# Attention features and a gated network on one core: the matrix S loaded as 16 columns and spread on the chip, values with 33 columns a head, a new order

## The chip, the cores and the metric

The kernel runs on one core of one Trainium2 chip. The metric is the device time in microseconds (us) of one execution, the median of three runs. Engines are PE (TensorE, matmuls), DVE (VectorE), ACT (ScalarE), POOL (GpSimd) and SP (SyncE, which issues most transfers).

## The reference, cut to what matters

```python
B, H, S, D = 4, 4, 1088, 32          # q, k, v: (B, H, S, D); S1, S2: (8, 32)
def phi(x):                          # 64 features of a row of 32
    a = np.einsum('rd,bhsd->bhsr', S1, x)
    b = np.einsum('rd,bhsd->bhsr', S2, x)
    return np.einsum('bhsi,bhsj->bhsij', a, b).reshape(*x.shape[:-1], 64)
q_p, k_p = phi(q), phi(k)
kv = np.einsum('bhsf,bhsd->bhfd', k_p, v)
z = np.sum(k_p, axis=2)
attn = np.einsum('bhsf,bhfd->bhsd', q_p, kv) / (np.einsum('bhsf,bhf->bhs', q_p, z)[..., None] + 1e-06)
x = attn.transpose(0, 2, 1, 3).reshape(4352, 128)
xn = x / np.sqrt(np.mean(x * x, axis=-1, keepdims=True) + 1e-06) * rms_g
g = xn @ w_gate                      # w_gate, w_val: (128, 1536); w_out: (1536, 128)
out = (g / (1 + np.exp(-g)) * (xn @ w_val)) @ w_out
```

S1, S2 and the weights come as 64-bit floats and are made into 32-bit ones on the chip.

## The kernel before, in words

The 4352 tokens are nine chunks (eight of 512, one of 256). For each of the four batches `kside(b)` projects the keys with S, takes the outer products of the two projections (`phi`, 64 features a head), and sums features times values into `kv` (line 531, the key-value products). The values `vt` have VA = 34 columns a head: 32 values, a one (its sum is z), and a zero. Batch 0 does this in groups of 1, 3, 3 and 2 key tiles of 128 rows: key products on PE (L519), a copy by ACT (`both`, L344), the outer product by POOL or DVE (L452), then L531. Batches 1 to 3 project turned (L497, four strips of 32 columns side by side on PE).

For each chunk `qside(c)` does the same with queries: chunks 0 and 1 with L594, the outer product into `at` (L452), transposes on PE (L602) and a copy into `phiq`; later chunks with L622 and a way through DRAM (`far`). Then come the numerator and denominator (L678), the division and the mean of squares on DVE, a power on POOL (`rstd`), the scaling of x on ACT or DVE, transposes on PE (L758), and the split of x into x_hi and x_lo.

A slot (c, j) is 128 of the 1536 hidden columns for one chunk: three matmuls each for the gate `g_ps` and the value `v_ps` (L802: x_hi with w_hi and w_lo, x_lo with w_hi), a silu on ACT into `s`, h = v*s on DVE, h split into h_hi and h_lo, and three matmuls into `o_ps` (L840). `weights(j)` loads 384 KB of 64-bit weights, casts the upper parts (`w_top`, L401), joins them (`w_full`, L396) and splits them (`w_hi`, `w_lo`). Gate and value have two banks each; `att` has three and `o_ps` one.

S as the kernel needs it, `sblk`, is block-diagonal: 128 rows (head and d), 64 columns (head, S1 or S2, r), zeros outside a head's own block. The host writes all of it, as 64-bit words; `to_f32` casts the upper halves (`s_top`) and joins them with the rest (`s_raw`) into `sblk`.

Nothing decides at run time. Every operation is a numbered task with one engine, or a choice of engines that the string `ON` makes; the list `ORDER` says in which sequence tasks are put down, and the numbers behind it (as LAGS, ASK, FETCH, FETCH_AT) are a model's from which slots of buffers and filler matmuls follow. Each engine runs its own instructions in that sequence. Fillers (L382) are products with zeros: eight at the start, and one wherever the model sees PE idle.

```python
load(P * NB * 16, lambda: nc.sync.dma_start(out=s_raw.bitcast(U16)[:, 1:4 * NB + 1], in_=sw.bitcast(U16)), ["s_raw"])
to_f32(NB, lambda: sblk, lambda: s_raw, lambda: s_top, ["s_raw", "table"], ["s_top"], ["sblk"])
```

Of the kernel before, what the change touches and what calls it, by code (L numbers as in the profile page):

```python
# [22 lines left out]
R = 8  # L23
F = R * R
NT = B * S
P = 128
# [9 lines left out]
VA = D + 2  # L36
# [3 lines left out]
LAGS = (210, 240, 740)  # L40
# [48 lines left out]
"""  # L89
ON = (  # L90
    "dapapadaddaadaadddaaaaapapdapapaadaadaadaapaadaadaadaadaddaadppddaapaadaaddadadadadadadadpdddaadddaaapapadadapapaadapapd"
    "dapapadapadapdpddddpadaaddadaapadaddpddadddadapadapddddadpadaadapaddpadapadddapapddadaaadpdaadpadadapddadddddapdpddddddd"
    "ddaaaapapapddapapdpdpddadaddpadadddaaaddddpapddadaddpadddapaddaddddaaddddpddapadadapadaddddpadpadddadadadadddapdda"
)
ATT = 3
# [856 lines left out]
```

## Time and profile before

| | |
|---|---|
| median of 3 runs | 252.21 us (252.2 to 252.3) |
| the profiled execution | 252.34 us, its span 250.4 us |
| busy in the span | PE 246.5, DVE 180.6, ACT 132.8, POOL 81.9 us |
| instructions | 5878 |
| moved by DMA | 25.55 MB, 20.40 MB read from HBM |
| first product with S, first up product, last product | starts at 4.21, 16.58 and 246.39 us (a group of eight, 1.05 us) |
| single durations on ACT | kv copy 0.21, copy of 512 columns 0.59, x_hi of 256 columns 0.46 us |
| single durations on DVE | join of 384 columns 0.55, kv copy 0.22, copy of 128 columns 0.28, eight columns 0.17 us |

The span runs from the first instruction to the last; the time has some 2 us around it. A timeline row is the start, the duration, the engine, the line, the operation, what it writes and reads, the shape, and how many records it covers; an idle time before it and what ended that stand in brackets. A 32-bit product is two records, and a product with rounded operands (hi or lo) one. A PE record reaches to the modelled end, so records overlap: the pace of PE is the distance from start to start.

### The profile page before, as it was taken

What the parts mean: (1) busy time and instruction counts of PE and PEld (TensorE: products, weight loads), DVE (VectorE), ACT (ScalarE), POOL (GpSimd) and SP (SyncE); (2) the same over time, 40 slices, a digit from 0 to 9 for tenths busy, and PEclk for the clock granted to TensorE, in tenths of its full rate; (3) what the DMA queues carried; (4) which work ended last, traced back from release to release, by engine and by line L of the source; (5) the groups of instructions that cost most, each with busy time, mean ns of one, the idle gap of its engine ahead of it and who ended that gap; (6) DMA issues with size and microseconds to landing.
All of it is one profiled execution on the core that took longest, in us unless ns stands there. A gap on an engine that the chain in (4) does not pass through costs nothing.

```text
span 250.4 us, 5878 instructions
## 1 busy us (share of the span) xinstructions
PE 246.5 (98%) x2244; PEld 198.7 (79%) x2244; DVE 180.6 (72%) x410; ACT 132.8 (53%) x287; POOL 81.9 (33%) x80
## 2 busy tenths in 40 slices
PE   8999999999999999999999999999999999999995
PEld 5977788777888788878888788888888888888894
DVE  1899998789467887575587678855678576765672
ACT  3686988564444747353445643553356464355351
POOL 4447031343664223223550403265332203132201
PEclk9999999999999999999999999999999999999999
DMA  6989892552371332321610254251002102010010
GB/s 238 359 265 343 269 251 91 158 152 45 108 205 41 86 98 77 105 86 34 183 34 1 47 153 112 45 149 61 3 0 46 41 3 43 21 63 3 0 42 21
DMA packets 19691, 25.55 MB, mean 102 GB/s; under 512 B 3152, under 2 KB 11472, under 8 KB 19664
## 3 DMA queue, kind: packets, MB, share of 16 engines
q1 hardware_dynamic: 19232, 24.54, 33.3%
q10 hardware_dynamic: 432, 0.66, 0.7%
q8 instruction: 17, 0.28, 0.4%
q14 instruction: 10, 0.08, 0.1%
HBM read 20.40 MB, written 4.78 MB: 101 GB/s over the span
## 4 chain that ended last, share of the span: by engine, by line
PE 98%; DVE 0%; issue 0%
PE v_ps L802 29%; PE g_ps L802 29%; PE o_ps L840 28%; PE att L678 3%; PE att L531 2%; PE o_ps L382 2%; PE att L622 1%; PE o_ps L531 1%; PE att L594 1%; PE att L758 1%; PE att L497 1%; PE g_ps L678 0%; PE att L602 0%; PE v_ps L678 0%; PE att L821 0%; PE g_ps L519 0%
## 5 line engine op out<-in xcount | busy, mean ns | idle before, releaser
L811 ACT ACTIVATE s<-g_ps 128x512 f32<-128x512 f32 (+1 forms) x108 | 61.0, 574 | 71.4 <-PE g_ps L802 38.1
L814 DVE TENSOR_TENSOR h<-v_ps,s 128x512 f32<-128x512 f32 (+2 forms) x110 | 69.8, 647 | 40.0 <-PE v_ps L802 27.7
L832 POOL TENSOR_TENSOR h_lo<-h,h_hi 128x512 fp32r<-128x512 f32 (+1 forms) x42 | 52.9, 1267 | 104.5 <-DVE h_lo L832 43.9
L350 ACT CAST h_hi<-h 128x512 fp32r<-128x512 f32 (+1 forms) x70 | 41.3, 601 | 19.9 <-DVE h L814 17.4
L832 DVE TENSOR_TENSOR h_lo<-h,h_hi 128x512 fp32r<-128x512 f32 (+1 forms) x64 | 41.4, 652 | 5.5 <-ACT h_hi L350 3.6
L802 PE MATMUL v_ps<-x_hi,w_hi 128*128 128x512 f32 (+1 forms) x110 | 41.9, 381 | 0.0
L802 PE MATMUL g_ps<-x_hi,w_hi 128*128 128x512 f32 (+1 forms) x110 | 41.9, 381 | 0.0
L802 PE MATMUL v_ps<-x_hi,w_lo 128*128 128x512 f32 (+1 forms) x110 | 41.6, 378 | 0.0
L802 PE MATMUL g_ps<-x_hi,w_lo 128*128 128x512 f32 (+1 forms) x110 | 41.5, 378 | 0.0
L802 PE MATMUL g_ps<-x_lo,w_hi 128*128 128x512 f32 (+1 forms) x110 | 41.5, 379 | 0.0
L802 PE MATMUL v_ps<-x_lo,w_hi 128*128 128x512 f32 (+1 forms) x110 | 41.3, 378 | 0.0
L840 PE MATMUL o_ps<-h_hi,w_hi 128*128 128x512 f32 (+1 forms) x106 | 40.9, 386 | 0.0
L840 PE MATMUL o_ps<-h_hi,w_lo 128*128 128x512 f32 (+1 forms) x106 | 40.8, 385 | 0.0
L840 PE MATMUL o_ps<-h_lo,w_hi 128*128 128x512 f32 (+1 forms) x106 | 40.8, 385 | 0.0
L802 PEld LDWEIGHTS v_ps<-x_hi,w_hi 128*128 128x128 f32 x110 | 20.6, 188 | 5.0 <-DVE w_lo L436 0.5
L802 PEld LDWEIGHTS g_ps<-x_hi,w_hi 128*128 128x128 f32 x110 | 20.7, 188 | 4.6
L802 PEld LDWEIGHTS v_ps<-x_hi,w_lo 128*128 128x128 f32 x110 | 20.7, 188 | 4.3
L802 PEld LDWEIGHTS g_ps<-x_hi,w_lo 128*128 128x128 f32 x110 | 20.7, 188 | 4.3
L802 PEld LDWEIGHTS g_ps<-x_lo,w_hi 128*128 128x128 f32 x110 | 20.6, 188 | 4.2
L802 PEld LDWEIGHTS v_ps<-x_lo,w_hi 128*128 128x128 f32 x110 | 20.5, 188 | 4.1
L840 PEld LDWEIGHTS o_ps<-h_lo,w_hi 128*128 128x128 f32 x106 | 19.9, 188 | 4.4
L840 PEld LDWEIGHTS o_ps<-h_hi,w_hi 128*128 128x128 f32 x106 | 19.9, 188 | 4.2
(112 smaller groups left out, 246.9 us busy)
## 6 DMA issues: line engine op xcount, KB each, us to landing
w_raw<-w SPq DMA_DIRECT2D x12, 384.0 KB
bt<-far SPq DMA_DIRECT2D x24, 128.0 KB
at<-far SPq DMA_DIRECT2D x12, 256.0 KB
outT<-o_sb SPq DMA_DIRECT2D x16, 128.0 KB
q<-qT SPq DMA_DIRECT2D x7, 256.0 KB
turned<-xq SPq DMA_DIRECT2D x24, 64.0 KB
xt<-turned SPq DMA_DIRECT2D x6, 256.0 KB
vt<-v SPq DMA_DIRECT2D x4, 272.0 KB
```

Source lines behind the costliest of these rows:

```text
L350: "act": on_act(n, lambda: nc.scalar.copy(out=out(), in_=in_()), True),
L382: nc.tensor.matmul(out=warm[:1, :cols], lhsT=zeros[:, :1], rhs=zeros[:, :cols], start=True, stop=True)
L497: nc.tensor.matmul(out=pair[p]()[a * D:(a + 1) * D, :g], lhsT=sblk[p * HALF:(p + 1) * HALF, p * NB // 2:(p + 1) * NB // 2], rhs=kt()[p * H ...
L531: nc.tensor.matmul(out=kvv[r0:r0 + wide, h // 2, :], lhsT=phi()[:, t, h * F + f:h * F + f + wide], rhs=vt()[:, t, h, :], start=(t == 0 and ...
L594: nc.tensor.matmul(out=ab()[hf * HALF:(hf + 1) * HALF, t * HALF:(t + 1) * HALF], lhsT=q()[:, s1:s1 + HALF], rhs=sblk, start=True, stop=True,)
L622: nc.tensor.matmul(out=accs[p]()[a * D:(a + 1) * D, :m], lhsT=sab[rows, p].rearrange("p c o r -> p (c o r)"), rhs=q()[rows, a * m:(a + 1) ...
L678: nc.tensor.matmul(out=nv[n0:n0 + wide, t, p, :], lhsT=phi()[:, p, l0:l0 + wide], rhs=kvs[(s0 + l0) // S][:, p, :], start=True, stop=True,)
L802: nc.tensor.matmul(out=acc()[:, cs], lhsT=wt[:, j, i3, :], rhs=x()[:, cs], start=(i == 0), stop=(i == 2))
L811: act(n, lambda: nc.scalar.activation(out=s()[:, :n], in_=gps()[:, :n], func=AF.Silu), cols(gps, whole[0]), [s])
L814: cs.stop - cs.start, lambda cs=cs: nc.vector.tensor_tensor(out=h()[:, cs], in0=vps()[:, cs], in1=s()[:, cs], op=ALU.mult),
L832: eng.tensor_tensor(out=h_lo()[:, :n], in0=h()[:, :n], in1=h_hi().bitcast(F32)[:, :n], op=ALU.subtract)
L840: nc.tensor.matmul(out=o_ps()[:, :n], lhsT=wt[:, j, 2, :], rhs=x()[:, :n], start=first and i == 0, stop=last and i == 2,)
```

## The change

The host now sends S1 and S2 side by side, 16 columns for each of the 128 rows (the same 32 rows for each head): 16 KB instead of 64. The chip joins these 16 columns (`s_one`) and multiplies them, repeated for four heads, with `own`, which is one where the row belongs to the column's head and zero elsewhere. `own` is made by five memsets on DVE at the start. Values have 33 columns a head. All tasks behind the join have a number one higher, and the order, the choice of engines and some numbers of the model are new. The lines move by six to ten: L519 is L529, L531 L541, L594 L604, L602 L612, L622 L632, L678 L688, L497 L507, L758 L768, L802 L812.

```diff
-VA = D + 2
+VA = D + 1
-LAGS = (210, 240, 740)
+LAGS = (120, 240, 700)
...
 ORDER = """
-1 0 2 6 9 3 14 10 15 4 32 33 7 37 16 5 64 34 18 38 19 12 26 27 22 20 146 39 28 147 11 23 24 151 35 40 41 65 17 13 148 21 25 36 29 152 153 149 66 72
+1 0 2 3 4 7 15 16 17 11 10 19 8 12 38 33 23 20 21 34 27 24 35 18 25 39 40 6 66 28 5 67 22 36 29 14 68 37 71 13 41 73 69 42 74 26 70 65 30 31 32 80
...
-AHEAD, FETCHED, BLOCK, ASK, FETCH = 62, 210, 128, 2600, 2400
+AHEAD, FETCHED, BLOCK, ASK, FETCH = 62, 210, 128, 3300, 2800
+LATE = 150
...
-    s_raw = const.tile([P, 2 * NB + 2], U32, name="s_raw")
+    s_raw = const.tile([P, 4 * R + 2], U32, name="s_raw")
...
-    s_top = const.tile([P, NB], U32, name="s_top")
+    s_top = const.tile([P, 2 * R], U32, name="s_top")
+    s_one = const.tile([P, 2 * R], F32, name="s_one")
+    own = const.tile([P, H], F32, name="own")
+    nc.vector.memset(own, 0.0)
+    for h in range(H):
+        nc.vector.memset(own[h * D:(h + 1) * D, h:h + 1], 1.0)
...
-    load(P * NB * 16, lambda: nc.sync.dma_start(out=s_raw.bitcast(U16)[:, 1:4 * NB + 1], in_=sw.bitcast(U16)), ["s_raw"])
+    load(P * 2 * R * 16, lambda: nc.sync.dma_start(out=s_raw.bitcast(U16)[:, 1:8 * R + 1], in_=sw.bitcast(U16)), ["s_raw"])
...
-    to_f32(NB, lambda: sblk, lambda: s_raw, lambda: s_top, ["s_raw", "table"], ["s_top"], ["sblk"])
+    to_f32(2 * R, lambda: s_one, lambda: s_raw, lambda: s_top, ["s_raw", "table"], ["s_top"], ["s_one"])
+    dve(NB, lambda: nc.vector.tensor_tensor(
+        out=sblk.rearrange("p (h x) -> p h x", h=H), in0=s_one.unsqueeze(1).to_broadcast([P, H, 2 * R]),
+        in1=own.unsqueeze(2).to_broadcast([P, H, 2 * R]), op=ALU.mult,
+    ), ["s_one"], ["sblk"], True)
```

The order below is that of each engine's own instructions: line, operation, what it writes and reads, the shape, and how often. First the start of PE, before: after the fillers a key tile (`kt`), query blocks (`q_109` is chunk 0, `q_113` chunk 1) with fillers between them, and the other key tiles.

```order
L382 MATMUL o_ps_97<-const-float32-0.0 1x96
L519 MATMUL g_ps_124<-sblk,kt_106 64x64 x2
L382 MATMUL o_ps_97<-const-float32-0.0 1x32
L594 MATMUL att_130<-sblk,q_109 64x64 x4
L382 MATMUL o_ps_97<-const-float32-0.0 1x128
L594 MATMUL att_144<-sblk,q_109 64x64 x4
L519 MATMUL v_ps_151<-sblk,kt_106 64x64 x6
L519 MATMUL v_ps_162<-sblk,kt_106 64x64 x4
L519 MATMUL g_ps_170<-sblk,kt_106 64x64 x6
L594 MATMUL att_179<-sblk,q_113 64x64 x4
L594 MATMUL att_186<-sblk,q_113 64x64 x4
L602 MATMUL g_ps_193<-ident,at_149 128x128 x4
```

The same place now. Behind the last of these rows stand 15 more key-value products, the transposes of chunk 0, twenty key-value products, and only then the two query blocks of chunk 1.

```order
L388 MATMUL o_ps_104<-const-float32-0.0 1x128 x8
L529 MATMUL g_ps_132<-sblk,kt_113 64x64 x2
L529 MATMUL v_ps_137<-sblk,kt_113 64x64 x6
L604 MATMUL att_150<-sblk,q_116 64x64 x4
L604 MATMUL att_159<-sblk,q_116 64x64 x4
L529 MATMUL g_ps_165<-sblk,kt_113 64x64 x6
L529 MATMUL v_ps_174<-sblk,kt_113 64x64 x4
L541 MATMUL o_ps_183<-vt_120,phi_148 64x33
```

So the key tiles moved ahead of the queries, the fillers between them are gone, and the first sixteen key-value products stand ahead of the transposes; before, all 36 stood behind them. DVE's first instructions show the new step and who makes the first large product; before:

```order
L357 MEMSET mhalf 128x4
L404 CAST s_top<-s_raw 128x64
L396 SCALAR_TENSOR_TENSOR sblk<-s_raw,s_top 128x64
L452 TENSOR_TENSOR at_149<-att_130,both_141 128x512
L452 TENSOR_TENSOR at_149<-att_144,both_158 128x512
L452 TENSOR_TENSOR phi_138<-v_ps_162,both_177 128x512
```

DVE now (the cast of `s_top` stands on ACT, behind its table load):

```order
L371 MEMSET own 128x4
L373 MEMSET own 32x1 x4
L402 SCALAR_TENSOR_TENSOR s_one<-s_raw,s_top 128x16
L419 TENSOR_TENSOR sblk<-s_one,own 128x64
L462 TENSOR_TENSOR phi_148<-v_ps_137,both_155 128x768
L462 TENSOR_TENSOR at_189<-att_159,both_172 128x512
L346 COPY both_205<-att_150 128x128
L462 TENSOR_TENSOR at_189<-att_150,both_205 128x512
```

The features of tiles 1 to 3 (768 columns) moved from POOL to DVE, ahead of the query products, and one copy came from ACT. The second place is PE from the last numerators of chunk 0 to the first up product, before (`kt_207` are the keys of batch 1, `xn_361` the x of chunk 0):

```order
L678 MATMUL g_ps_328<-kv_73,phiq_284 64x66 x8
L678 MATMUL v_ps_346<-kv_73,phiq_284 64x66 x8
L622 MATMUL att_364<-q_198,sab 32x128 x4
L622 MATMUL att_369<-q_198,sab 32x128 x4
L497 MATMUL g_ps_382<-kt_207,sblk 32x288 x4
L497 MATMUL v_ps_387<-kt_207,sblk 32x288 x4
L758 MATMUL att_404<-ident,xn_361 128x128 x2
L382 MATMUL att_411<-const-float32-0.0 1x128
L758 MATMUL att_419<-ident,xn_361 128x128 x2
L802 MATMUL v_ps_424<-x_hi_415,w_hi 128x256
```

And now:

```order
L632 MATMUL att_366<-q_179,sab 32x128 x4
L768 MATMUL att_376<-ident,xn_354 128x128 x2
L507 MATMUL g_ps_387<-kt_157,sblk 32x288 x4
L507 MATMUL v_ps_392<-kt_157,sblk 32x288 x4
L632 MATMUL att_408<-q_280,sab 32x128 x4
L632 MATMUL att_413<-q_280,sab 32x128 x4
L812 MATMUL v_ps_420<-x_hi_400,w_hi 128x256
L812 MATMUL v_ps_420<-x_hi_400,w_lo 128x256
L812 MATMUL g_ps_429<-x_hi_400,w_hi 128x256
L812 MATMUL g_ps_429<-x_hi_400,w_lo 128x256
L768 MATMUL att_435<-ident,xn_354 128x128 x2
L812 MATMUL v_ps_420<-x_lo_418,w_hi 128x256
```

The x transposes moved ahead of the key projection, the filler is gone, and the second half of the transposes stands behind four up products. The third place is the key projection of batch 3 on PE; before, it stands alone between up products:

```order
L802 MATMUL g_ps_1029<-x_lo_530,w_hi 128x512
L497 MATMUL att_1037<-kt_740,sblk 32x288 x4
L497 MATMUL att_1042<-kt_740,sblk 32x288 x4
L802 MATMUL v_ps_1052<-x_hi_521,w_hi 128x512
L802 MATMUL v_ps_1052<-x_hi_521,w_lo 128x512
```

Now it opens a stretch of narrow products (`vt_613` are the values of batch 2):

```order
L812 MATMUL v_ps_1112<-x_lo_418,w_hi 128x512
L507 MATMUL att_1119<-kt_564,sblk 32x288 x4
L507 MATMUL att_1124<-kt_564,sblk 32x288 x4
L541 MATMUL att_1132<-vt_613,phi_821 32x33 x48
L688 MATMUL att_1186<-kv_75,phiq_1085 32x66 x16
```

It moved next to key-value products and numerators, whose products also lie in strips of 32 columns.

## Rows read from the trace of the kernel before

**Rows 1.** The chain that ended last, its shares of the span by engine.

```profile
PE 98%; DVE 0%; issue 0%
```

**Rows 2.** One stretch: its length, then busy us of each engine, granted clock, DMA share.

```profile
40.00:246.40 206.40, 206.40 (x1667) 167.46 (x1666) 147.99 (x329) 103.25 (x215) 64.70 (x51) 1.00 0.25 68
```

**Rows 3.** Timeline of the start: start, duration, engine, line, operation.

```profile
0.74 0.39 SPq L409 DMA_DIRECT2D s_raw<-sw  x1
0.77 3.47 PE L382 MATMUL o_ps<-const-float32-0.0 128*1 128x128 f32 x16 [0.77 <-PEq L945]
...
2.95 0.20 ACT L410 ACTIVATE spare<-mhalf 128x4 f32<-128x4 f32 x1
...
3.69 0.21 DVE L404 CAST s_top<-s_raw 128x64 f16<-128x64 bf16 x1 [2.82 <-DMA s_raw<-sw]
...
3.93 0.23 DVE L396 SCALAR_TENSOR_TENSOR sblk<-s_raw,s_top 128x64 uint32<-128x64 uint32 x1
...
4.21 0.48 PE L519 MATMUL g_ps<-sblk,kt 128*64 128x64 f32 x4
```

**Rows 4.** Timeline of the first feature products, 4.8 to 10 us.

```profile
4.81 0.70 PE L594 MATMUL att<-sblk,q 128*64 128x64 f32 x8
...
5.82 0.45 PE L594 MATMUL att<-sblk,q 128*64 128x64 f32 x8
...
6.10 0.75 PE L519 MATMUL v_ps<-sblk,kt 128*64 128x64 f32 x20
...
7.13 1.51 POOL L452 TENSOR_TENSOR phi<-both 128x768 f32<-128x768 f32 x1 [1.47 <-ACT both L344]
...
7.61 0.66 PE L602 MATMUL g_ps<-ident,at 128*128 128x128 f32 x4
7.98 0.32 ACT L344 COPY both<-g_ps 128x192 f32<-128x192 f32 x1 [0.22 <-DVE phi L452]
...
8.33 0.96 DVE L452 TENSOR_TENSOR phi<-g_ps,both 128x768 f32<-128x768 f32 x1 [0.39 <-ACT both L344]
...
8.63 0.24 PE L531 MATMUL o_ps<-vt,phi 128*64 128x34 f32 x1
...
9.80 0.68 DVE L452 TENSOR_TENSOR at<-att,both 128x512 f32<-128x512 f32 x1
```

**Rows 5.** Timeline of PE from the numerator to the first up product.

```profile
11.44 0.69 PE L678 MATMUL g_ps<-kv,phiq 128*64 128x66 f32 x16
...
13.49 0.69 PE L678 MATMUL g_ps<-kv,phiq 128*64 128x66 f32 x16
...
14.58 0.45 PE L622 MATMUL att<-q,sab 64*32 64x128 f32 x16
14.82 0.42 PE L497 MATMUL g_ps<-kt,sblk 64*32 64x288 f32 x4
...
15.44 0.44 PE L758 MATMUL att<-ident,xn 128*128 128x128 f32 x2
15.81 0.38 PE L382 MATMUL att<-const-float32-0.0 128*1 128x128 f32 x2
16.34 0.41 PE L758 MATMUL att<-ident,xn 128*128 128x128 f32 x2 [0.15 <-PE att L382]
16.58 0.39 PE L802 MATMUL v_ps<-x_hi,w_hi 128*128 128x256 f32 x1
```

**Rows 6.** Timeline of PE around two changes of tile shape.

```profile
54.70 0.39 PE L802 MATMUL g_ps<-x_lo,w_hi 128*128 128x512 f32 x1
55.03 0.72 PE L497 MATMUL att<-kt,sblk 64*32 64x288 f32 x16
55.67 0.50 PE L802 MATMUL v_ps<-x_hi,w_hi 128*128 128x512 f32 x1
...
61.14 1.44 PE L531 MATMUL att<-vt,phi 128*32 128x34 f32 x144
62.42 1.13 PE L678 MATMUL att<-kv,phiq 128*32 128x66 f32 x64
```

More of the change, by code (lines that the diff above doesn't have):

```diff
@@ L53 @@
 ORDER = """
[35 rows of a table removed]
[35 rows of a table added]
 """
 ON = (
-    "dapapadaddaadaadddaaaaapapdapapaadaadaadaapaadaadaadaadaddaadppddaapaadaaddadadadadadadadpdddaadddaaapapadadapapaadapapd"
-    "dapapadapadapdpddddpadaaddadaapadaddpddadddadapadapddddadpadaadapaddpadapadddapapddadaaadpdaadpadadapddadddddapdpddddddd"
-    "ddaaaapapapddapapdpdpddadaddpadadddaaaddddpapddadaddpadddapaddaddddaaddddpddapadadapadaddddpadpadddadadadadddapdda"
+    "aapadapadadadaddaaaaaaaddpdapadaadaadaadaadaadaadaapaapaapdadpppaaapaadaadaadadadadadadaddddadadpaadadadadadapddaadadada"
+    "dadadapadapapadapddpddaadddddadaddpdpdpaddpapapapdddpadapddddapdddpadapdpadapddadapaddaadddaddddpapadddapddadadadadapaaa"
+    "ddadaadadapapapapdpadadadapdpdadpdaddaddpadapddddddapdpdddpdddaappdadddpddddddddapddapdpapddaadddaddpadapadapapdda"
 )
@@ L110 @@
 OTHER = 300
-AHEAD, FETCHED, BLOCK, ASK, FETCH = 62, 210, 128, 2600, 2400
+AHEAD, FETCHED, BLOCK, ASK, FETCH = 62, 210, 128, 3300, 2800
+LATE = 150
 STALL = (3200, 0)
-FETCH_WIRE, FETCH_AT = 1300, (9800, 16300, 26400, 31000)
+FETCH_WIRE, FETCH_AT = 1100, (9750, 15200, 24500, 32000)
 COLD = (5600, 1.5)
@@ L236, in follow @@
             if e == "dma":
-                begin = max(wire, at + FLIGHT + OTHER * (w.since > 0))
+                begin = max(wire, at + FLIGHT + LATE + OTHER * (w.since > 0))
                 wire = begin + w.lat
@@ L889, in attention_then_glu @@
     global PLAN
-    PLAN = plan, plan.run({"pe": 3760, "act": 1600, "dve": 1000, "pool": 2000, "dma": 740}, keep_warm, lambda: nc.cur_bb.bb.instructions)
+    PLAN = plan, plan.run({"pe": 3760, "act": 1600, "dve": 1400, "pool": 2000, "dma": 740}, keep_warm, lambda: nc.cur_bb.bb.instructions)
     def tie(ins, other, how):
@@ L924, in _layout @@
     qT = np.ascontiguousarray(q.transpose(1, 3, 0, 2)).reshape(H * D, NT)
-    sblk = np.zeros((H, D, H, 2, R), np.float64)
-    for h in range(H):
-        sblk[h, :, h, 0] = S1.T
-        sblk[h, :, h, 1] = S2.T
-    return kT, va, qT, _words(sblk.reshape(H * D, H * 2 * R))
+    s_all = np.concatenate([np.asarray(S1, np.float64).T, np.asarray(S2, np.float64).T], axis=1)
+    return kT, va, qT, _words(np.concatenate([s_all] * H))
 def kernel(q, k, v, S1, S2, moe_w_gate, moe_w_val, moe_w_out, moe_rms_g):
```

68 rows, old and new, of the table ORDER are left out of this document.

## The prediction

> **What bounds the kernel now.** I read the chain of waits first, then the stretches, then the timeline of the first 17 us. In the chain [rows 1] TensorE (PE) holds 98% of the span and no other engine has a share: from some point on, the end is a sum of matmuls. The row of the stretch 40 to 246.4 us [rows 2] shows PE busy in all 206.4 us of it while VectorE (DVE) has 148. Busy alone could hide waits, since a matmul's record may contain one, so the starts matter: the steps of the up and down products of 512 columns start 0.23 apart [rows 6], and after 16.6 us the listed PE rows leave that pace only where the tile shape changes. So a change can pay in three ways: the slots start sooner, PE has fewer or shorter things to do after that, or the tail is shorter. The tail (the last four small products and the store) has the same operations in both kernels; I give it nothing.
>
> The start is what the reader should look at next. DVE waits for the load of S until 3.69, converts and joins it, and the first product starts at 4.21 [rows 3]. From there PE is fed by feature products: the one of key tiles 1 to 3, 768 columns on GpSimd (POOL), starts at 7.13 and takes 1.51, and as it ends, at 8.63, the key-value products start [rows 4]. They occupy PE until the numerator starts at 11.44, 0.6 us of transposes included. Then PE works through numerators, query and key projections to 15.81, has only a filler and a gap until 16.34, and starts the first up product at 16.58 [rows 5]. After that it never waits.
>
> **The change, part by part.**
>
> *Load and blocks of S.* The load shrinks from 64 to 16 KB. At the rate of the start, about 0.37 MB/us, 48 KB are worth 0.13 us at most and nothing at least; I take 0.13, so the data is seen at 3.56. Then three instructions instead of two: a cast on ScalarE (ACT), at least the 0.20 of its smallest activation, a join of 16 columns on DVE (0.17 to 0.23; the 64-column one took 0.23, its cast 0.21), and the new product with ones and zeros over 64 columns, nowhere in the trace; the nearest row, the 64-column join, gives 0.23, and between nothing and twice that I take it. With three hand-overs of 0.04: 3.56 + 0.20 + 0.18 + 0.23 + 0.12 = 4.29, against 4.21 [rows 3]. The bounds are 4.2 (the fillers now last to there) and 4.5. The five small memsets on DVE lie in its wait before 3.69 and cost nothing; without that cover they would cost some 0.3 us.
> [...] The new rows are 128 B where the old ones were 512 B. [...]
>
> *First products, anew.* I walk PE through its new order with the old durations. Early matmuls are slow: eight records of the query block took 0.70 at 4.81 and 0.45 at 5.82 [rows 4]; a key tile took 0.12 later (five in 0.59, 6.10 to 6.69), and I take 0.24 for it before 5.6. PE: four key tiles 4.29 to 5.25, two query blocks to 6.05, five key tiles to 6.65. Results reach ACT 0.2 after the last start. ACT copies tiles 1 to 3 (0.32) by 5.8, and DVE, not POOL, makes their product (0.96): 5.8 to 6.76. The key-value products of tiles 0 to 3 therefore start near 6.8 instead of 8.63. Sixteen of them at 0.062 (36 took 2.2 us) and their first tile ahead: to 7.75. DVE makes the two query products (0.68 each, with a 0.28 copy between): 7.4 and 8.25. Transposes (0.5 each) to 8.25 and 8.8. POOL has tiles 4 to 6 by 8.45 (copy to 6.9, then 1.51); twenty key-value products to 10.1; the two query blocks of chunk 1, which stood ahead of them before, to 10.6. By then both kv copies (0.2) are done. So the numerator starts near **10.6 against 11.44**. DMA does not forbid it: the load of S is smaller, chunk 1's queries now travel behind values and weights, and the bytes up to the first values are fewer (1.1 MB against 1.35).
>
> *On to the first up product.* Here work that stood earlier comes due. DVE: kv copy, weight join (0.55), query product (0.68), to 11.7; POOL makes the other to 12.15. PE: two numerators to 11.65, transposes 11.75 to 12.75. ACT copies them (0.59 each) by 13.55. PE: two numerators (1.09) to 14.15, first possible end; query projection 0.4 to 14.55, x transposes 0.37 to 14.95, key projection 0.62 to 15.55, second query projection 0.4: up product at **15.95 against 16.58** [rows 5]. ACT turns x into x_hi meanwhile (0.46, by 15.6). The gain is 0.63, but half of the x transposes now comes after the first four up products and costs PE 0.28, which before lay in the gap. **Term 1: -0.35**, between +0.1 (every queue of that stretch a little late) and -0.85 (the lead of 0.84 kept to the end).
>
> *Fewer changes of tile shape.* Before, the third key projection stands alone between up products [rows 6]: entered 0.09 late (54.70 + 0.23 to 55.03), 0.64 long, and the first step after it 0.11 longer than 0.23. In the new order it stands together with key-value products and numerators, which pay entry and exit anyway. After the first up product the order has eight such excursions instead of nine. **Term 2: -0.20** (0.1 to 0.3).
>
> *33 columns.* 36 groups of four key-value products took 1.28 us [rows 6], 36 ns for 34 columns; the numerators' 16 groups of 66 columns lasted 1.13 with the end of the last, some 60 ns each. That is 0.7 ns a column and group; three batches of 36 give **term 3: -0.07**, bounds 0 and -0.12 (in proportion to the columns). [...] The first batch, 62 ns a pair, I leave at nothing. The value loads lose 3%, 18 KB, under 0.05 us of a transfer that PE does not wait for.
>
> *Order after the start.* Same products, other sequence; PE was fed without a wait before, with DVE at 148 of 206 us [rows 2], and I take it that it stays so. The tightest place that I find is rival D.
>
> Sum: -0.35 - 0.20 - 0.07 = -0.62. The profiled execution took 252.34, so 251.72; the median of the runs is 0.13 lower, which gives **251.6**.
>
> **Rivals.**
> A, the forecast: 251.3 to 251.9.
> B, the lead is kept whole: the numerator's 0.84 is carried to the first up product (15.7), because ACT and DVE keep pace. For it: PE ends each stretch of the walk with little idle time. Against: the two transposes that now come after the numerator wait for DVE and POOL. -0.85 - 0.27 = -1.1: 251.1.
> C, the lead is lost between numerator and first up product: ACT has kv copy, two small copies, two of eight columns, a weight cast, two copies of 512 columns and the two x products in one file there; each 0.1 late counts. Up product at 16.3 to 16.6, then terms 2 and 3 alone with the moved transposes: -0.2 to +0.1, about 252.1.
> D, slower: the change of banks after the first slots. The second v product of slots 2 and 3 takes the bank that DVE frees only after a silu on ACT, and that silu stands behind a weight cast which waits for a join on DVE, behind x_lo and two means. In my walk the bank is free at 21.0 and wanted at 21.45. PE idles for all beyond 0.42, and past 1.05 us of lateness the whole gain is gone; DVE is nearly always busy there. At 1.7 late: 252.9.
> E, the load is no sooner: the first product at 4.42 to 4.6 and all behind it until the numerator 0.13 to 0.3 later, as PE and DVE follow each other closely there: 251.75 to 251.9. [...]
>
> **Chances.** No change and a change of 0.2% (0.5 us) cannot be told apart here, so faster means below 251.7. A 0.42 (0.32 of it below), B 0.15, C 0.17 (all within), D 0.16, E 0.10 (0.02 below). Faster 0.49, within 0.35, slower 0.16. The likeliest case has 251.3 to 251.9; the range that leaves out no more than most of D and the end of B is 250.8 to 252.6.
>
> **What would show it.** First product at 4.2 to 4.4; key-value products from 6.8, in two pieces; numerator near 10.6; first up product near 15.95, the same steps of 0.12 and 0.23 behind it; no PE start gap over 0.35 after that outside tile changes; eight excursions; the span near 249.8. Wrong would be: a filler-like gap of PE in 20 to 25 us (D), the first up product after 16.3 (C), or S seen after 3.7 (E).

## The result, and the profile after

The changed kernel took **254.16 us** (median of 6 runs, 253.17 to 254.79) against 252.25 (6 runs, 252.03 to 252.44): ratio 1.0071, 95% interval 1.0046 to 1.0096. It is slower by 1.9 us and outside the predicted range. The profiled execution took 254.79 with a span of 253.1, against 252.34 and 250.4. The ratios below leave out two slow runs, 256.95 of e8 and 261.94 of e10.

The chain that ended last, its shares by engine, answers to [rows 1]:

```profile
PE 94%; DMA 4%; issue 1%; SPq 0%; DVE 0%
```

Before, PE held 98%. "issue" is time in which an engine waited for nothing that the profile shows; DMA is the start, where PE now waits for the queries of chunk 1. The waits of PE, in the columns engine, line, what it waited for, us in total, times, the longest:

```profile
PE att L688 <- issue: 1.9, 1, 1.9
...
PE o_ps L541 <- DMA vt<-v: 0.2, 1, 0.2
PE att L604 <- DMA q<-qT: 0.2, 1, 0.2
```

One wait of 1.9 us, as long as the whole loss. Its place, in PE's timeline (it answers to the second half of [rows 6]):

```profile
61.01 0.72 PE L507 MATMUL att<-kt,sblk 64*32 64x288 f32 x16
61.66 1.02 PE L541 MATMUL att<-vt,phi 128*32 128x33 f32 x95
...
62.49 0.44 PE L688 MATMUL att<-kv,phiq 128*32 128x66 f32 x16
64.80 0.38 PE L688 MATMUL att<-kv,phiq 128*32 128x66 f32 x12 [1.86 <-issue]
...
65.03 0.64 PE L541 MATMUL att<-vt,phi 128*32 128x33 f32 x46
...
65.48 0.66 PE L688 MATMUL att<-kv,phiq 128*32 128x66 f32 x31
66.08 0.49 PE L812 MATMUL g_ps<-x_hi,w_hi 128*128 128x512 f32 x1
```

PE stops in the middle of a numerator, between two products of one line that read the same `kv` and `phiq`; 17 of its 32 records are done and 15 still to come. No semaphore, operand or bank changes there. The windows ahead of and in the gap (length, busy us of PE, PEld, DVE, ACT, POOL, granted clock, DMA share, GB/s) show that the others work on and the clock is full:

```profile
60.00:62.90 2.90, 2.90 (x134) 1.85 (x132) 2.18 (x5) 0.60 (x2) 1.28 (x1) 1.00 0.36 95
62.90:64.80 1.90, 0.04 (x4) 0.01 (x2) 1.58 (x3) 0.60 (x1) 0.94 (x1) 1.00 0.02 2
```

What PE lacks, as the experiments below show, is instructions. The page's queues have one kind called "instruction":

```profile
PE 247.0 (98%) x2238; PEld 199.6 (79%) x2238; DVE 181.6 (72%) x414; ACT 129.4 (51%) x272; POOL 86.0 (34%) x85
...
q8 instruction: 17, 0.28, 0.5%
```

17 transfers of 16 KB for 2238 records of PE: one for about 128 records (e7 and e10 below have 32 records more and 18 transfers). Each is one packet. In the 0.2 us from 62.3 the trace has one of them, which lasts from 62.33 to 63.45, beside packets of the four stores `turned<-xq`:

```profile
q1 hardware_dynamic: 79, 0.04, 70.3%
q8 instruction: 1, 0.02, 34.9%
```

PE goes on at 64.80, 1.35 after the end of this transfer.

The start (ACT, DVE and PE), answering to [rows 3 to 5]:

```profile
3.37 0.21 ACT L407 CAST s_top<-s_raw 128x16 f16<-128x16 bf16 x1 [0.22 <-DMA s_raw<-sw]
...
3.83 0.22 DVE L419 TENSOR_TENSOR sblk<-s_one,own 128x64 f32<-128x64 f32 x1
...
4.28 0.48 PE L529 MATMUL g_ps<-sblk,kt 128*64 128x64 f32 x4
...
7.20 0.21 PE L541 MATMUL o_ps<-vt,phi 128*64 128x33 f32 x1 [0.22 <-DMA vt<-v]
...
10.80 0.69 PE L604 MATMUL att<-sblk,q 128*64 128x64 f32 x16 [0.16 <-DMA q<-qT]
11.29 0.67 PE L688 MATMUL g_ps<-kv,phiq 128*64 128x66 f32 x16
...
16.60 0.38 PE L812 MATMUL v_ps<-x_hi,w_hi 128*128 128x256 f32 x1
```

The key-value products start 1.43 sooner (7.20 for 8.63), the numerator 0.15 sooner (11.29 for 11.44), the first up product no sooner (16.60 for 16.58).

### The profile page after: what moved, and what is told of

Its sections match the earlier page's. It is cut to its first block, busy times and chain, and to the rows that moved or that the text cites. A ratio compares the mean times of both kernels' runs of the same rounds, so it can differ in the third digit from the quotient of the medians.

```text
span 253.1 us, 5860 instructions
## 1 busy us (share of the span) xinstructions
PE 247.0 (98%) x2238; PEld 199.6 (79%) x2238; DVE 181.6 (72%) x414; ACT 129.4 (51%) x272; POOL 86.0 (34%) x85
## 4 chain that ended last, share of the span: by engine, by line
PE 94%; DMA 4%; issue 1%; SPq 0%; DVE 0%
PE g_ps L812 29%; PE v_ps L812 28%; PE o_ps L850 28%; DMA q<-qT 4%; PE att L688 3%; PE att L541 2%; PE att L632 1%; PE att L507 1%; PE att L612 0%; PE g_ps L688 0%; PE v_ps L688 0%; PE att L768 0%; PE att L831 0%; PE att L604 0%; PE g_ps L507 0%
## 5 line engine op out<-in xcount | busy, mean ns | idle before, releaser
L842 POOL TENSOR_TENSOR h_lo<-h,h_hi 128x512 fp32r<-128x512 f32 (+1 forms) x44 | 54.3, 1243 | 111.2 <-DVE h_lo L842 46.2
L351 ACT CAST h_hi<-h 128x512 fp32r<-128x512 f32 (+1 forms) x69 | 40.3, 596 | 14.7 <-DVE h L824 12.2
L842 DVE TENSOR_TENSOR h_lo<-h,h_hi 128x512 fp32r<-128x512 f32 (+1 forms) x62 | 40.6, 659 | 4.6 <-ACT h_hi L351 3.0
L812 PE MATMUL g_ps<-x_hi,w_hi 128*128 128x512 f32 (+1 forms) x110 | 42.1, 383 | 0.0
L812 PE MATMUL v_ps<-x_hi,w_hi 128*128 128x512 f32 (+1 forms) x110 | 42.0, 382 | 0.0
L812 PE MATMUL v_ps<-x_lo,w_hi 128*128 128x512 f32 (+1 forms) x110 | 41.6, 378 | 0.0
L812 PE MATMUL g_ps<-x_hi,w_lo 128*128 128x512 f32 (+1 forms) x110 | 41.5, 377 | 0.0
L812 PE MATMUL v_ps<-x_hi,w_lo 128*128 128x512 f32 (+1 forms) x110 | 41.4, 377 | 0.0
L812 PE MATMUL g_ps<-x_lo,w_hi 128*128 128x512 f32 (+1 forms) x110 | 41.4, 378 | 0.0
L812 PEld LDWEIGHTS g_ps<-x_hi,w_hi 128*128 128x128 f32 x110 | 20.6, 188 | 5.2 <-ACT w_hi L351 0.5
L812 PEld LDWEIGHTS v_ps<-x_hi,w_hi 128*128 128x128 f32 x110 | 20.6, 188 | 4.5 <-ACT xn L741 0.2
L812 PEld LDWEIGHTS v_ps<-x_lo,w_hi 128*128 128x128 f32 x110 | 20.6, 188 | 4.3
L812 PEld LDWEIGHTS g_ps<-x_lo,w_hi 128*128 128x128 f32 x110 | 20.6, 188 | 4.3
L812 PEld LDWEIGHTS g_ps<-x_hi,w_lo 128*128 128x128 f32 x110 | 20.6, 188 | 4.2
L812 PEld LDWEIGHTS v_ps<-x_hi,w_lo 128*128 128x128 f32 x110 | 20.6, 188 | 4.2
```

What stands on the lines that cost most here:

```text
L351: "act": on_act(n, lambda: nc.scalar.copy(out=out(), in_=in_()), True),
L812: nc.tensor.matmul(out=acc()[:, cs], lhsT=wt[:, j, i3, :], rhs=x()[:, cs], start=(i == 0), stop=(i == 2))
L842: eng.tensor_tensor(out=h_lo()[:, :n], in0=h()[:, :n], in1=h_hi().bitcast(F32)[:, :n], op=ALU.subtract)
```

## The theory and its rivals

**Theory 1, instruction supply.** I counted PE's records in the trace from 0. Where the trace shows nothing that it waited for, PE stops only behind certain numbers: 853, and in other runs below 981, 983, 1236 and 1493, all 128 or a multiple apart to within a few. I take the transfer ahead of each stop to bring what follows it. The one for 853 never starts more than 0.7 us before record 715 does, so I use that record as its mark. The order decides which products those are. Before, the third key projection, 16 quick records, stood ahead of record 715; now it stands behind it, in one stretch with key-value products and numerators. So record 715 starts 1.65 later (58.59 for 56.94), and from it to record 853 PE takes 4.13 us where it took 5.12. Narrow products are quick: 95 records in 0.83 us from 61.66 on, 9 ns each, where an up product takes 230.

**Rivals.** 2: the data changes (16 columns of S, 33 columns a head) cost the time and the order nothing. 3: the four stores `turned<-xq`, issued at 59.9 and moving from 60.7 on, when the transfer should, delay it; sooner stores would cure it. 4: the loss is at the start, and the gap only a trait of the one profiled execution.

## The experiments

Each is compared with runs of the kernel before that were taken beside it. An ORDER edit shows only the task numbers that move.

**e1_data_only and e2_order_only: the change in two halves.** e1 is before's ORDER and planner numbers with the new S and VA = D + 1; e2 the new order with the old S and VA = D + 2.

```diff
 # e1, in before
-VA = D + 2
+VA = D + 1
+    to_f32(2 * R, lambda: s_one, lambda: s_raw, lambda: s_top, ["s_raw", "table"], ["s_top"], ["s_one"])
...
 # e2, in after
-VA = D + 1
+VA = D + 2
...
```

> The order, the choice of engines and the planner's numbers of before; S spread on the chip and values of 33 columns as in the change. Theory 1 (PE runs out of instructions in the new order, since a 16 KB instruction transfer comes late in the stretch of narrow products at 60 to 66 us): no idle PE in that stretch, 252.0 to 252.3 us, that is before within 0.1%. Rival (the changed data path itself costs the time): 253.5 to 254.5 us, with a later first up product or longer key-value products.

> The new order with S loaded whole and values of 34 columns as before. Theory 1: the idle 1 to 2 us of PE in the numerators near 62 to 65 us is there again, 253.2 to 254.8 us. Rival (data path): 252.0 to 252.6 us.

e1: 252.44 (12 runs) against 252.24, ratio 1.0018 (0.9999 to 1.0036), 0.14 above the range expected of it. e2: 254.8 (6 runs), ratio 1.0103 (1.0064 to 1.0141), as expected. The order carries the loss, the data at most a few tenths (the interval ends at 0.9 us); rival 2 falls as the main cause. One caution: e2's profiled execution was its quickest, 252.98, and has no gap. Its transfer came at 60.38, 2.2 behind record 715, and PE just got through. So the gap probably comes in some executions and not in others; one execution alone of each run has a profile.

e1 also prices term 3 by itself. In its timeline a key-value batch of 36 groups is

```profile
61.07 1.43 PE L541 MATMUL att<-vt,phi 128*32 128x33 f32 x144
62.35 0.37 PE L688 MATMUL att<-kv,phiq 128*32 128x66 f32 x10
```

1.28 from start to start with 33 columns, and 1.28 with 34 [rows 6]: nothing saved.

**e3_narrow_later: the narrow stretch behind two slots' products.** The tasks 417 to 444, the key projection, key-value products and numerators of that place, stand some 1.4 us of wide products later; nothing is left out.

```diff
-351 417 237 418 419 239 450 394 395 241 444 355 356 383 278 344 362 363 385 384 386
+351 394 395 355 356 383 278 344 362 363 385 384 417 237 418 419 239 450 241 444 386
```

> After with the stretch of narrow products (key projection, key-value products and numerators of 61 to 66 us) put behind the next gate and value product, 1.4 us of wide products. Theory 1: PE reaches the instructions of the late transfer 1.4 us later, so its idle time shrinks from 1.86 to 0.3 to 0.7 us or is gone; 252.4 to 253.6 us. Rival (the numerators wait for a buffer or an operand of their own): the idle time stays at 1.5 to 2 us in the same numerators, 253.8 to 254.8 us.

252.77 (252.24 to 253.83, 12 runs), ratio 1.0012 (0.9986 to 1.0038): no loss clear of the noise is left, by moving wide products ahead of narrow ones. In its trace the transfer starts at 58.51, 0.03 behind record 715, and the numerator runs through:

```profile
64.16 0.66 PE L688 MATMUL att<-kv,phiq 128*32 128x66 f32 x31
64.62 0.60 PE L541 MATMUL att<-vt,phi 128*32 128x33 f32 x46
```

**e4_turned_early: the stores issued sooner (rival 3).** Task 274, the DVE transpose ahead of the four stores, stands behind 273.

```diff
-273 392 391 353 373 442 360 443 331 393 274 343
+273 274 392 391 353 373 442 360 443 331 393 343
```

> After with one step of VectorE (the turning of xn into xq) put ahead of two others, so that the four stores of xq to DRAM are issued some 1.5 to 2 us earlier than at 59.9 us; PE's order is unchanged. Theory 1a (the instruction transfer queues behind these stores): it starts near 60.5 instead of 62.3 us, the idle time is under 0.3 us, 252.3 to 253.2 us. Theory 1b (the transfer is late for another reason): it starts near 62.3 as it did, the idle time stays at 1.5 to 2 us, 253.2 to 254.8 us.

254.1 (6 runs), ratio 1.0082 (1.0052 to 1.0112). The stores were issued at 58.73 instead of 59.90, and the transfer still came at 62.08, with 1.82 idle. Rival 3 falls. Its profiled execution, the longest at 256.15, shows a second price:

```profile
64.66 0.38 PE L688 MATMUL att<-kv,phiq 128*32 128x66 f32 x12 [1.82 <-issue]
...
66.43 0.63 PE L812 MATMUL g_ps<-x_hi,w_lo 128*128 128x512 f32 x1
66.85 0.63 PE L812 MATMUL g_ps<-x_lo,w_hi 128*128 128x512 f32 x1
```

Up products start 0.43 apart instead of 0.23, and the windows give the clock:

```profile
66.00:70.00 4.00, 4.00 (x12) 3.13 (x12) 0.69 (x1) 1.45 (x3) 0.52 (x1) 0.57 0.63 208
70.00:74.00 4.00, 4.00 (x19) 3.23 (x18) 3.63 (x6) 2.33 (x6) 0.00 (x0) 1.00 0.70 209
```

The granted clock is 0.57 over 66 to 70, with steps of 0.43 up to 69.4; 12 products where 4.00 / 0.23 would be 17, so (17 - 12) x 0.23, by my estimate some 1.2 us, are lost. In after's own profile the clock stays 1.00 over the same window, behind a gap as long.

**e5_after_again: the changed kernel once more, without an edit.**

> The changed kernel once more, as it is, to see whether the idle time is a property of its order. Theory (instruction transfer late in this order): a profile shows PE idle behind the same record of the numerators again, if the transfer starts after 61.5 us, and no idle time if it starts before 60.5; 253.2 to 254.8 us, and a run that adds a low clock behind the idle time 256 or more. Rival (a chance disturbance of one profile): no idle time, and times within 0.3% of before.

254.66 (253.19 to 255.21, 6 runs), ratio 1.0081 (1.0052 to 1.0110); transfer at 62.24, 2.14 idle behind record 853. The gap is in the second profile too, as expected; rival 4 falls as far as the gap goes.

**e6_one_product_ahead: half of e3.** Narrow tasks behind 383, 0.70 us later.

```diff
-351 417 237 418 419 239 450 394 395 241 444 355 356 383
+351 394 395 355 356 383 417 237 418 419 239 450 241 444
```

> As e3, but only one product of three passes (0.70 us) stands ahead of the narrow stretch instead of two. Theory (PE stops at the first record of a block that has not come, until 1.2 to 1.35 us after the transfer's end): if the transfer starts at 62.1 to 62.3 as in the changed kernel, PE is idle for 1.1 to 1.3 us, 253.0 to 254.0 us; if it starts at 58 to 60.5, as in e3 and e2, not at all, 252.4 to 253.2 us. Rival (each wide product ahead has no say): idle 1.8 to 1.9 us.

254.34 (253.29 to 256.2, 9 runs), ratio 1.0062 (1.0035 to 1.0089). Record 853 starts at 64.78, the transfer only at 64.22: 1.89 idle, as without the move and as the rival of this run said. The dose I had counted on, some 0.7 us of slack for 0.7 us of wide products, is not there: the transfer came later too (4.23 behind record 715, which starts at 59.99). So the move doesn't shorten the gap in proportion; in these profiles the supply is either prompt or late.

**e7_shift_32: records put in, the order left.** 16 one-column products with zeros, 32 records, ahead of batch 3's key projection, so that every later record has a number 32 higher. The real product there writes over what they leave.

```diff
+                for _ in range(16 * (b == 3)):
+                    nc.tensor.matmul(out=pair[0]()[:1, :1], lhsT=zeros[:, :1], rhs=zeros[:, :1], start=True, stop=True)
```

> After with sixteen products of one column with zeros (32 records) put ahead of the key projection of that stretch, into a bank that the projection overwrites; all else in the same order. Theory (instructions come in blocks; PE stands at a fixed count of records): the idle time is behind the same record of PE, number 853, which is now a key-value product (L541), 30 to 34 records sooner in the work than before, and ends 1.2 to 1.4 us after the transfer's end; 253.6 to 255.4 us. Rival (the numerators wait for something of their own): the idle time stays in the numerators, 17 records behind their start.

256.59 (256.02 to 257.17, 6 runs), ratio 1.0166 (1.0141 to 1.0190). PE's timeline:

```profile
64.60 0.50 PE L814 MATMUL g_ps<-x_hi,w_hi 128*128 128x512 f32 x1
66.47 0.40 PE L814 MATMUL g_ps<-x_hi,w_lo 128*128 128x512 f32 x1 [1.38 <-issue]
```

The gap leaves the numerator and opens between two up products of one bank, behind record 981, with the next block's transfer at 63.76 to 64.89; a second one, 1.09, lies behind record 1236. I had expected it behind 853 and at most 255.4: a miss, since here the transfer for 853 was prompt (58.35) and PE stopped at the ends of later blocks. But the gap follows the number of the record, 128 further on, not the operation: no wait for data would do that. This is the strongest single piece for theory 1.

**e10_before_32: the same records in the kernel before.**

```diff
+                for _ in range(16 * (c == 5)):
+                    nc.tensor.matmul(out=accs[0]()[:1, :1], lhsT=zeros[:, :1], rhs=zeros[:, :1], start=True, stop=True)
```

> The kernel before with sixteen products of one column with zeros (32 records) ahead of the query projection that opens its own narrow stretch at 61 us; order and all else as before. Theory (128 records a transfer; the stretch now ends at record 981 instead of 949): PE is idle behind record 981, in the first wide products after the stretch, near 65 us, for 0.8 to 1.6 us, though the order is that of before; 253.8 to 255.5 us (0.7 of it the added products). Rival (only the new order has such idle times): no idle time, 252.8 to 253.2 us.

258.86 (258.04 to 261.94, 7 runs), ratio 1.0226 (1.0183 to 1.0269). The old order, which had no gap, now has two, behind records 983 and 1493 (PE's waits):

```profile
PE att L680 <- issue: 3.0, 1, 3.0
PE att L531 <- issue: 2.1, 1, 2.1
```

Behind the first, the granted clock was 0.66 from 70 to 74. I had expected one gap of 0.8 to 1.6 and at most 255.5; the sign was right, the size a miss. So a kernel can be without the gap by the luck of where its narrow stretches stand. (The profiled execution was its longest, 261.94; the other six took 258.04 to 259.66, and that they have these gaps is inferred. In this one PE also waits 1.4 for queries at the start.)

**e11_key3_alone: undo term 2 alone.** The third key projection stands alone between up products again.

```diff
-390 273 392 391 353 373 442 360 443 331 393 274 343 338 361 439 351 417 237 418 419 239
+390 417 418 419 273 392 391 353 373 442 360 443 331 393 274 343 338 361 439 351 237 239
```

> After with one thing of its order put back: the key projection of batch 3 (sixteen records, 0.65 us) stands alone between up products at 55.5 us, as it did before, instead of opening the narrow stretch at 61; its two turnings on VectorE move with it. Theory: record 715, with which the transfer of the block behind record 853 starts at the earliest (56.94 in before, 58.59 in the changed kernel), comes near 56.2 again, PE reaches 853 near 62.8 as it did, and a transfer late by up to 4 us still comes in time: no idle time, 252.5 to 253.1 us, though a change of tile shape (0.2 to 0.3 us) is paid again. Rival (the transfer is late in this order wherever record 715 lies, or something else holds PE): idle 1.8 to 2.1 us behind record 853, 254 to 255 us.

253.13 (252.71 to 253.99, 12 runs), ratio 1.0024 (1.0006 to 1.0042). Record 715 is back at 57.42, the transfer prompt (56.79), and PE runs through:

```profile
62.19 1.03 PE L541 MATMUL att<-vt,phi 128*32 128x33 f32 x96
63.07 0.67 PE L688 MATMUL att<-kv,phiq 128*32 128x66 f32 x32
```

No run reached 254, where after's median lies. The move that was to save 0.2 us was what cost the gap. What is left, 0.75 us by the medians, was the subject of the next.

**e12_silu_first: e11, and a silu ahead of a weight cast.** In e11 PE waits at 27.7 for a bank, and ACT shows why (both timelines):

```profile
27.71 0.50 PE L812 MATMUL g_ps<-x_hi,w_hi 128*128 128x512 f32 x1 [0.56 <-ACT s L821]
```

```profile
25.57 1.13 ACT L407 CAST w_top<-w_raw 128x384 f16<-128x384 bf16 x2 [0.91 <-DMA w_raw<-w]
26.57 0.61 ACT L351 CAST h_hi<-h 128x512 fp32r<-128x512 f32 x1
27.08 0.58 ACT L821 ACTIVATE s<-g_ps 128x512 f32<-128x512 f32 x1
```

The silu stands behind casts that wait 0.91 for weights. Before, the silu (25.16) stood ahead of them (25.65). In e12 it stands between the two.

```diff
-91 282 92 96 204 284 97
+91 282 92 204 284 96 97
```

> As e11, and on ScalarE one of the two weight casts at 25 us put behind the silu of the same time, which frees the bank of the gate product at 27 us (0.56 us idle in e11, behind a weight load that came 0.9 us late). Theory: this wait of PE shrinks by the cast's 0.5 us to 0.1 or nothing, and the time by 0.2 to 0.5 from e11's 253.13, to 252.6 to 252.9 us, not below before, since the first up product is no sooner. Rival (the bank waits for something else): the wait stays, 253.0 to 253.3 us.

253.07 (252.43 to 253.68, 9 runs), ratio 1.0034 (1.0018 to 1.0049). The wait is gone from its profile, whose span is 0.65 shorter than e11's (251.14 for 251.79) although its first up product comes 0.46 later (16.73 for 16.27). Yet the median moved 0.06 only and lies in the range of this run's rival. The 0.8 us left isn't this wait alone.

**e8_q1_first: chunk 1's queries ahead of weights 1.** Load task 65 stands ahead of 73.

```diff
-41 73 69 42 74 26 70 65 30
+41 65 73 69 42 74 26 70 30
```

> After with the load of chunk 1's queries (256 KB) put ahead of the second weight load (384 KB). Theory for the start (PE's lead was lost to two loads, 0.4 us to the values at 7.2 and 0.3 to these queries at 10.45): PE does not wait for the queries, the numerator starts at 11.0 instead of 11.29, and the first up product 0 to 0.3 sooner than 16.60, less what the later weights delay on VectorE; 253.2 to 254.8 us with the idle time at 62 us unchanged. Rival (the engines behind, not the loads, hold the numerator): it stays at 11.2 to 11.4.

254.18 (252.5 to 256.95, 12 runs), ratio 1.0048 (1.0017 to 1.0078). The start:

```profile
10.12 0.66 PE L604 MATMUL att<-sblk,q 128*64 128x64 f32 x16
...
11.36 0.45 PE L688 MATMUL g_ps<-kv,phiq 128*64 128x66 f32 x8 [0.26 <-DVE kv L566]
```

Chunk 1's queries are no longer waited for, and the numerator comes no sooner, as the rival of this run said: the kv copy on DVE is now the last to end (10.98 to 11.21), as a weight cast two places ahead of it waits 0.78 for the weights that now come later. The load only moves the wait. The gap stays (1.83 idle in its profile), and five runs of 252.5 to 253.4 beside seven of 254 and more suggest that it comes in some executions only; that is inferred, since one execution alone has a profile.

**e9_split: e3 in two pieces,** the last three tasks a little later still; they are taken from where e3 takes them.

```diff
-385 384 386 345 424
+385 384 417 237 418 419 239 386 345 450 241 444 424
```

> After with the narrow stretch put two products later, as in e3, and cut in two: key projection and the first 96 records of key-value products, one down product (0.70 us), then numerators, the other key-value products and numerators. Theory: record 853 is reached only at 64.5 us or later, and a transfer that starts as late as 62.3 has been worked off by then, so no run has an idle time; 252.6 to 253.2 us (one more change of tile shape, some 0.3 us) and no run above 253.8. Rival (idle times come with the new order at any place): runs of 254 and more stay.

253.25 (252.53 to 255.14, 12 runs), ratio 1.0024 (0.9999 to 1.0048). Two runs of 254 and more, where I had put none above 253.8: a miss. Its profile doesn't show why; there the transfer is prompt (58.26). Its start shows rival C by itself:

```profile
10.72 0.67 PE L688 MATMUL g_ps<-kv,phiq 128*64 128x66 f32 x16
...
14.33 0.69 PE L688 MATMUL g_ps<-kv,phiq 128*64 128x66 f32 x16 [0.51 <-ACT w_hi L351]
...
16.56 0.38 PE L812 MATMUL v_ps<-x_hi,w_hi 128*128 128x256 f32 x1
```

The numerator is nearly where the walk put it (10.6), and the lead is gone 5.8 us later.

## Why the prediction was wrong, step by step

The supply in all profiled executions, by the trace's records and packets (the idle time as far as the modelled end of record 853 shows it; by starts it is some 0.2 longer):

| kernel | record 715 starts | transfer | record 853 starts | idle behind it |
|---|---|---|---|---|
| before | 56.94 | 56.89 to 57.83 | 62.06 | none |
| e1 | 56.88 | 56.78 to 57.90 | 61.99 | none |
| e11 | 57.42 | 56.79 to 58.07 | 63.30 | none |
| e12 | 56.81 | 56.69 to 57.62 | 62.69 | none |
| e3 | 58.48 | 58.51 to 59.68 | 64.29 | none |
| e9 | 58.11 | 58.26 to 59.21 | 64.92 | none |
| e10 | 58.43 | 58.22 to 59.15 | 64.16 | none (3.00 a block later) |
| e7 | 58.34 | 58.35 to 59.61 | 62.97 | none (1.38 a block later) |
| e2 | 58.15 | 60.38 to 61.40 | 62.72 | none (a step of 0.16) |
| after | 58.59 | 62.33 to 63.45 | 62.72 | 1.86 |
| e4 | 58.49 | 62.08 to 63.45 | 62.62 | 1.82 |
| e5 | 58.57 | 62.24 to 63.63 | 62.70 | 2.14 |
| e6 | 59.99 | 64.22 to 65.55 | 64.78 | 1.89 |
| e8 | 57.43 | 61.91 to 63.21 | 62.45 | 1.83 |

**The step that failed** is "Order after the start. Same products, other sequence; PE was fed without a wait before ... I take it that it stays so." I had priced the feeding of PE by data, banks and engines, and not by instructions. Whatever lies between record 715 and 853 hides the transfer, and this cover has a size. A prompt transfer ends 0.6 to 1.3 after record 715 starts, and PE goes on 1.2 to 1.6 after the end of one that it had to wait for (64.80 after 63.45; 66.47 after 64.89 in e7), 2.4 to 3.0 after its start; before had 5.12 us to cover it, after has 4.13. Both would do, were the transfer always prompt. In after it started 3.7 behind record 715, and 3.7 + 2.5 is past 4.13 by 2.1, the distance from 62.72 to 64.80; as late a one would be past the 5.12 of before by 1.1.

The rows for this stood in the profile before: the page's instruction queue (17 transfers, 0.28 MB, as after), and PE's 5 us between those records. The diff named it as well: the planner's BLOCK of 128 records, and its ASK and FETCH, raised from 2600 and 2400 to 3300 and 2800, are a model of this supply (its FETCHED, 210, and 5 x 128 make 850, three short of 853). I read them as numbers that nothing on the chip obeys, which is true, and did not ask what they model.

The trace of after has 17 transfers of 16 KB for 2238 records of PE, each record a load of weights (PEld x2238) and a product. What a late one costs I take from the runs.

**Term 1 (-0.35) measured about 0.** The start of S agreed, 4.28 where I had 4.29, but by luck. The load was seen at 3.37, 0.32 sooner than before and not 0.13 at most (the 64 KB of e2 at 3.46), and `sblk` was done at 4.05; then PE was still at the last of its eight fillers, of 128 columns. In e1, where that one has 64 columns, `sblk` was done at 3.95 and the first product starts at 4.06. So the load did gain, and the longer filler took it; rival E did not happen. The key-value products came at 7.20 instead of 6.8 (0.22 of it a wait for values), the numerator at 11.29 instead of 10.6 (chunk 1's queries 0.16 of it; in e8, without that wait, the kv copy takes their place), and the up product at 16.60 instead of 15.95. The walk timed PE, DVE and ACT, and let loads be in time because there were fewer bytes; e9 shows that even with the numerator at 10.72 the lead is lost by 16.56, with 0.51 in a wait for ACT. That is nearest to rival C, which had 0.17.

**Term 2 (-0.20): right in itself, and the trigger.** I compared starts with the usual pace (0.2335 for 512 columns). From 52.6 to 56.7, where before pays 0.21 to enter and leave the lone key projection, after pays nothing, and it has eight excursions for nine. But batch 1's key-value products take 1.83 in the new order (29.38 to 31.21) and took 1.56 before (27.53 to 29.09), 0.27 more:

```profile
27.53 1.62 PE L531 MATMUL att<-vt,phi 128*32 128x34 f32 x144
29.09 0.51 PE L840 MATMUL o_ps<-h_hi,w_hi 128*128 128x512 f32 x1
...
29.38 1.91 PE L541 MATMUL att<-vt,phi 128*32 128x33 f32 x144
31.21 0.50 PE L812 MATMUL v_ps<-x_hi,w_hi 128*128 128x512 f32 x1
```

(The first two rows are before's, the others after's.)

Why is not settled (e12 had 1.51). And the move put the record count where the supply could fail: e11 undoes it and the gap is gone.

**Term 3 (-0.07) measured 0**, by e1: side by side the products go at 9 ns each (144 records in 1.28 us), with 33 columns as with 34. The 0.7 ns a column was my estimate from products of 34 and of 66 columns; why this one column saves nothing is not shown.

**Rival D** (slower, 0.16) had the sign and a mechanism that exists, but at 27 to 29 us and not at 20 to 25, and worth 0 to 0.75 in the profiles (0.05 in after, 0.75 in e6). It does not explain the result.

**The sum.** After's profile has a span 2.64 longer than before's: 0.02 up to the first up product, 2.08 for the gap by starts (62.72 to 64.80), 0.46 otherwise up to the last product, 0.08 behind it. Of the 0.46, 0.27 are batch 1's key-value products; the remainder I could not place. So without the gap the profile would still be 0.56 longer, where I had put 0.62 shorter. The medians agree as far as they go: e11, without the gap in its profile, is 0.75 above before, and after's quickest run, 253.17, some 0.9; that the latter has no gap is inferred.

**What stays open:** why the transfer is prompt in one execution and 2 to 4.5 us late in another. It isn't the four stores (e4). From 58.4 to 60.7 after's DMA moves nothing, so it isn't queued behind bytes there; between record 715 and the packet the trace shows nothing. Record 715 is a mark, not a shown trigger: it doesn't tell e7, with 4.63 us between the two records and a prompt transfer, from e6, with 4.79 and a late one.

The place of the narrow stretch in the block does tell them apart. The block that ends with 853 begins near record 726. In the five late profiles the stretch's first product in strips of 32 columns is record 725 (after, e4, e5), 728 (e6) or 729 (e8), and the transfer starts 1.1 to 1.3 behind that product; in the eight prompt ones the stretch begins at 731 or later (757 in e7), and in e2, in between, at 727. So where the change to strips falls in the block may have a say in when the transfer starts; how is not shown, and no run was made to test it.

The kernel before may meet the gap too: 8 of its 91 runs beside these experiments took 253.5 or more, none of them profiled. Two of them (254.88 and 255.04) have a mean granted clock of 0.993, where its other runs have 0.998 or more; e4's and e10's profiles, with 0.992 and 0.993, have the low clock behind a gap. No version that I made beats the kernel before.

## What to carry to other kernels

An order of instructions has a supply of its own. On PE, count records in blocks of 128 (the stops seen here lie behind 853, 981, 983, 1236 and 1493) and look where a stretch of narrow products meets the end of a block: side by side they use a block up in little over a microsecond (9 ns a record), and the slowest transfer seen here, 4.5 us behind record 715 and 2.5 more until PE went on, needs 7 us of products to hide, which neither kernel has at that place (5.12 before, 4.13 after). Wide products among them lengthen the cover (5.81 in e3). A wait that the view puts down to "issue" in the middle of one line's products may be this, and putting a few tiny products ahead tests it: the gap goes by the record number (from 853 to 981 in e7). A lead at the start is worth only what reaches the first long run of products (in e9 0.72 at the numerator, 0.02 at the up product), so walk it with loads and weight splits, not with bytes alone.

## What the runs showed of the hardware

- PE's instructions arrive during the run in 16 KB transfers, those of the table 0.9 to 1.4 us long, and where PE had to wait it went on 1.2 to 1.6 us after the end. The table's transfers started between 0.7 before and 4.5 us after record 715.
- 32 records of nothing (e10) raised the median by 6.35 us (252.51 to 258.86); the longest run's profile has two gaps of 3.0 and 2.1 and the clock at 0.66 over 4 us behind the first.
- In e4 a gap of 1.8 us was followed by 3.4 us of steps of 0.43 instead of 0.23 (66.0 to 69.4, the granted clock 0.57 over 66 to 70); in after a gap as long by none (1.00).
- A key-value product of 33 columns costs what one of 34 does, 36 ns for four records side by side (e1 and before, 1.28 us for 144).
